# An attention kernel planned at build time: new times in its planner, a drain time between dependent passes, queued broadcasts, and a table of leads by query block

## The chip, the cores and the metric

The kernel runs on one core of a Trainium2 chip. The metric is the device time of one execution in microseconds (us). Before the change the median of three runs is 408.36 us (408.36 to 408.42).

## The reference

Multi-head attention over one sequence of 2048 tokens, 16 heads of 28 columns, bfloat16 inputs:

```python
B, S, D, H = 1, 2048, 448, 16
qkv = (lambda x, *d: x.transpose(*d))((x @ wqkv).reshape(B, S, 3, H, Dh), 2, 0, 3, 1, 4)
q, k, v = qkv[0], qkv[1], qkv[2]
scores = jnp.einsum("bhqd,bhkd->bhqk", q, k) * (Dh ** -0.5)
p = _softmax(scores, axis=-1)
o = jnp.einsum("bhqk,bhkd->bhqd", p, v)
return (lambda x, *d: x.transpose(*d))(o, 0, 2, 1, 3).reshape(B, S, D) @ wo
```

## The kernel before

**Tiling.** The heads form 4 groups of 4 (g), the queries 4 chunks of 512 (c), the keys 16 tiles of 128 (j). A *query block* w = 4g + c is one chunk of one group; there are 16. A *score tile* is 128 keys by 512 queries of one head; there are 16 x 16 x 4 = 1024. Four score tiles (the heads of a group) with the same j make a *row*. TensorE (PE) computes the scores transposed, keys on the partitions (`emit_S`, L868), so that the exponentials can be fed back as they are: for each row four matmuls with a 32-column weight, side by side in the array, add V times exp into the bank PO (`pv_op`, L1136). A column of ones in VA gives the softmax's sum. Instead of a row's maximum, a bound of it is folded into the scores with extra partitions of Q and K (KMAX, NK, KPART, QP).

**Three ways to an exponential.** PSUM has eight banks: two pairs PA (two tiles each), three single banks PD, and PO.
- ACT: two score tiles in a PA pair, one Exp over 1024 columns into PTA (L1291).
- DVE with GpSimd (POOL): one score tile in a PD bank; DVE makes DU (L1072) and DV (L1075), POOL the product DG (L1078), DVE adds it up to the bits of the exponential in PTD (L1091). The PD bank is free after the last of them. Here this is called a DVE tile.
- POOL alone: DVE copies the bank to SG (L1004), POOL does six operations on it (L1011 to L1034). There are 24 such tiles; `ahead` takes them from some rows ahead of the others.

**Other work between them.** PE also makes K (L525), Q (L656) and V (L727) of the next group or query block and the output projections (L810, L830, L902, L1430). DVE copies these from PSUM. DMAs on SP's queue copy Q and K to other partitions (QB<-QB, QB<-QP, KB<-KB) and broadcast the key bound (KB<-NK); after each query block the sums go out and come back as a broadcast (DCO, SCR, RRB), and POOL divides (OT, L971). At the start x is transposed on PE (L417) or by DMA, and copied to XT (L428, L430).

**What sets the order.** Nothing is ordered by hand. At build time the kernel plays its own execution through: every piece of work is an `Op` with an engine, a planned duration, a latency until others may use the result, dependencies, and a priority. A loop steps through planned time. For each engine it takes the next Op (`try_pe`, `try_act`, `try_static`) and appends it to a log, which then becomes the program: one fixed queue for each engine, whose instructions wait for semaphores at run time. So the planned durations decide the order, and also which score tile goes to ACT and which to DVE, since a tile goes to DVE whenever a PD bank is planned to be free. The real times are the chip's.

In `try_pe` the order of choice is: scores for ACT when a PA pair is free; a late projection; a score tile for DVE when a PD bank is free; a PV row; another projection; otherwise a matmul of zeros to keep PE busy. Each of the later choices must pass `fits`: it may not hold PE past the end of the running exp by more than `SLK`. A matmul of another family (scores, PV, projections) than the last is charged `MODE`.

```python
def fits(dur, fam):
    d = dur + (MODE if fam != last_fam[0] else 0.0) + (MODE if fam != "S" else 0.0)
    return not tight or not any(t < x and t + d > x + SLK for x in exp_ends)
```

Projections have a position of the score tiles from which they may run (`elig`), a priority (`due`), and one from which they may also take a PD bank (`urgent`). The constants `UK`, `UQ`, `LA`, `J0`, `O1`, `O2`, `OF`, `RV`, `GY`, `GS` and others give these leads, the same for all query blocks.

Of the kernel before, what the change touches and what calls it, by code (L numbers as in the profile page):

```python
# [10 lines left out]
ALU = mybir.AluOpType  # L11
# [10 lines left out]
G = 4  # L22
HG = 4
# [16 lines left out]

SEM = 0.13
MM = 0.22
MODE = 0.105
PLAT = 0.24
P1 = 0.598
TT5 = 0.33
TS5 = 0.2
PTT = 1.12
PTS = 0.59
PST = 1.125  # L50
CPY = 0.6
EVK = 0.66
RED = 0.59
DISS = 0.6
DLAT = 1.4
QLAT = 2.6
# [26 lines left out]
def kernel(  # L83
# [31 lines left out]
    UK = 30  # L115
# [3 lines left out]
    LA = 10  # L119
# [3 lines left out]
    GY = 0.5  # L123
    GS = 1.0
    GBEG = 40
    J0 = 10
    NTAIL = 8
    JL = 6
    JACC = 8
    DI = 1  # L130
    PVM = 0.0
    PLD = 0.2
    YIELD = 0
    SLAT = 0.5
    ASL = -0.05
    ELAT = 0.05
    PGAP = 0.03
    PFIN = 0.3
# [3 lines left out]
    RNGB = 6.2  # L142
    RNGN = 0.35
    J3 = 9
    UQ = 60
    OD = 2
    PADQ = 1
    O1 = 10
    O2 = 20
    OF = 0.4  # L150
    RV = 2
    QPR = 100
    LOOK = 0.2
    SLK = 0.13
    MG = 0.1
# [7 lines left out]
    UO = 40  # L163
    FB = TPC
    NF = 2
    J1 = 8
# [189 lines left out]

    def step():
        pos[0] += 1
        while pos[0] in taken:
            pos[0] += 1  # L360
# [26 lines left out]
    k0mm = []  # L387
    hot = []
# [13 lines left out]
    for b in range(NQC - XBAR):  # L402
        xs_in = add(Op("SP", 0.01, None, prio=-2000 + b, lat=XLAT[b]))
        for hf in range(2):
# [14 lines left out]
            tro = add(Op("PE", 0.55 if b else (0.75, 0.65)[hf], tr, deps=[xs_in], prio=(-1200 if b else -5000) + 10 * b + (hf ^ THF[b]), lat=PLAT, kind="T",  # L419
# [66 lines left out]
    k0mv = []  # L486
    m0 = Op("DVE", 0.0, None)
# [23 lines left out]
    def task_K(g, sc):  # L511
        due = g * 4 * WT - 200 + 36 * sc
# [5 lines left out]
        else:  # L518
            task = bank_task()
            acq = acq_d(task, urgent=(g - 1) * 4 * WT + (sc + 1) * KSP - UK)  # L520
            elig = at((g - 1) * 4 * WT + sc * KSP + 2)
            prio = due
        def ap():
# [3 lines left out]
                       (xt_done[sc] if g or sc else xt_done[0][:1]) + [w_ready[("k", g)]], prio, elig, acq, half=None if g or sc else xt_done[0][1:])  # L527
        if g == 0 and sc == 0:
            k0mm.extend(ops)
        cs = slice(sc * QW, (sc + 1) * QW)  # L530
        if g == 0:
# [18 lines left out]
            else:  # L550
# [6 lines left out]
                evs[0].acq = lambda t: red.start is None or red.done(t)  # L557
# [13 lines left out]
    def task_kmax(g):  # L571
# [7 lines left out]
        if g == 0:  # L579
            nk = add(Op("DVE", 0.2, lambda: nc.vector.tensor_scalar(  # L580
                out=NK[0][:], in0=maskm[:, 0:P], scalar1=KMAX[0][:, 0:1], scalar2=RK0[:, 0:1], op0=ALU.mult, op1=ALU.mult),
                deps=[m] + rk_op, prio=prio + 0.2))
            for n, (c0, c1) in enumerate(KCH):
                for i in range(HG):
# [3 lines left out]
                        deps=[k0ev[sc] for sc in range(c0, c1)], prio=-2000 + 20 * n + i, lat=DLAT + 0.3))  # L588
# [8 lines left out]
            for n, (c0, c1) in enumerate(RCH):  # L597
                for i in range(HG):
                    o = add(Op("SP", DISS + 0.07, (lambda i=i, c0=c0, c1=c1: rep0(i, c0, c1)), deps=[nk],
                               prio=(-1990 + 20 * n if c0 else -300) + 0.1 * i, lat=DLAT + 0.6, elig=None if c0 else lambda t: pos[0] >= NF * FB * HG + 4))  # L600
                    for c in range(c0, c1):
                        kmrep[(g, c, i)] = o
# [3 lines left out]
        for st in (1, 3):  # L606
            o = add(Op("SP", DISS, (lambda st=st: nc.sync.dma_start(
                out=KB[g % 2][1][HP * st:HP * (st + 1), c0 * QW:S], in_=KB[g % 2][0][HP * st:HP * (st + 1), c0 * QW:S])),
                deps=[kev[(g, sc, 0)] for sc in range(c0, NQC)], prio=due + 0.01 * st, lat=DLAT + 0.3))
# [11 lines left out]
        for i in (2, 3, 0, 1):  # L621
            o = add(Op("SP", DISS + 0.07, (lambda i=i: rep_out(i, c0)), deps=[nk] + ([deps[i]] if i < 2 else []),
                       prio=due + 0.3 + 0.001 * i, lat=DLAT + 0.6))
# [7 lines left out]
    def task_Q(g, c):  # L631
# [9 lines left out]
        else:  # L641
            task = bank_task()
            acq = acq_d(task, urgent=w * WT - UQ)
            elig = at((w - 1) * WT + 3 - (QEA if w > 3 else 0))
            prio = due - (QPR if w > 3 else 0)
# [71 lines left out]
    def task_V(g, jq):  # L717
        due = g * 4 * WT + jq * TPC * HG - 12 + (FB * HG * (NF - 1) if g == 0 and jq else 0)
        task = bank_task()
        early = False  # L720
        elig = at(VE + jq * 5 if g == 0 else (g - 1) * 4 * WT + jq * WT + 4)
# [8 lines left out]
        for jj in range(TPC):  # L730
            ops.append(add(Op("PE", 0.27, (lambda jj=jj: mm(jj)), deps=(xt_done[jq] + [wvin]) if jj == 0 else [ops[-1]],
                              prio=prio + 0.001 * jj, kind="W", elig=elig, acq=acq_d(task, early, urgent=due - UV if g == 0 else (g - 1) * 4 * WT + (jq + 1) * WT + 32) if jj == 0 else None,
                              lat=0.0 if jj < TPC - 1 else PLAT)))
# [9 lines left out]
        ev = add(Op(eng, 0.54, ev_fn, deps=[ops[-1]], prio=prio - (0 if early else 1000), elig=elig))  # L743
# [43 lines left out]
    def task_part(c, n):  # L787
        due = (12 + c) * WT - PARTD
# [678 lines left out]
```

## Time and profile before

| | |
|---|---|
| median of three runs | 408.36 us |
| the profiled execution, its own time | 408.52 us |
| its span, first to last instruction | 406.7 us |
| granted PE clock, mean | 0.999 |
| DVE passes L1072, L1075, L1091 | 158 each; mean 680, 681, 679 ns |
| POOL DG L1078 | 158, mean 1154 ns |
| copies to SG L1004 | 24, mean 682 ns |
| score matmuls L868 to PA, to PD | 842, 182 |
| PV matmuls L1136 | 1024 |
| busy: PE, DVE, ACT, POOL | 89%, 94%, 97%, 82% of the span |

How to read it: a group's line gives the source line, the engine, the operation and what is written from what is read, then the count, the busy time, the mean of one record and the idle time of the engine just before such instructions. Records of one engine overlap, because an engine begins an operation while the last one drains; the mean of one record is therefore longer than the step from one to the next. In a timeline the two numbers in front are the start and the length, both in us, and square brackets hold the engine's idle time before, with what ended it.

### The profile page before, as it was taken

The numbers are of one execution on the slowest core, as the hardware profiler recorded it, in microseconds if no ns is written. First come the engines' busy times: TensorE is split into PE (matmuls) and PEld (weight loads), VectorE is DVE, ScalarE is ACT, GpSimd is POOL, SyncE is SP. The second block draws the span as 40 slices with busy tenths as digits, with TensorE's granted clock in tenths as the row PEclk, the third lists the DMA queues.
The fourth block names the chain that finished last, engine by engine and source line by source line (L and its number), as shares of the span: only waits on it lengthen the run. The fifth ranks groups of instructions, "written<-read, shape, count | busy, mean of one in ns | idle before, by whom it ended". The sixth has DMA issues, their size and how long they took to land.

```text
span 406.7 us, 7593 instructions
## 1 busy us (share of the span) xinstructions
PE 362.2 (89%) x2606; PEld 121.4 (30%) x2606; DVE 381.5 (94%) x671; ACT 393.6 (97%) x432; POOL 331.5 (82%) x357
## 2 busy tenths in 40 slices
PE   8999888898998989899898989899898888989896
PEld 5243232323222222222323223232322222222232
DVE  6998999999999999989999998999989999999995
ACT  4989999999999999999999999999999999999994
POOL 4038799678699899998989898898898889999860
PEclk9999999999999999999999999999999999999999
DMA  9351130211400002100510000010130101000112
GB/s 219 44 86 39 48 76 3 50 27 28 96 5 27 19 24 35 16 25 6 110 30 27 23 4 26 2 47 21 48 59 15 35 1 46 22 20 10 47 73 90
DMA packets 36446, 16.58 MB, mean 41 GB/s; under 512 B 28784, under 2 KB 33136, under 8 KB 36408
## 3 DMA queue, kind: packets, MB, share of 16 engines
q1 hardware_dynamic: 35800, 15.89, 16.7%
q8 instruction: 20, 0.33, 0.3%
q10 hardware_dynamic: 608, 0.22, 0.2%
q14 instruction: 18, 0.15, 0.1%
HBM read 7.44 MB, written 1.97 MB: 23 GB/s over the span
## 4 chain that ended last, share of the span: by engine, by line
ACT 74%; PE 16%; issue 7%; DVE 1%; ACTq 0%
ACT PTA L1291 74%; PE PA L868 6%; PE PO L1136 4%; PE PD L868 1%; PE PD L810 1%; PE PA L396 1%; PE PO L810 1%; PE PD L417 1%; DVE DU L1072 0%; DVE DV L1075 0%; PE PO L525 0%; PE PD L525 0%; PE PA L417 0%; PE PD L902 0%; PE PD L656 0%
## 5 line engine op out<-in xcount | busy, mean ns | idle before, releaser
L1291 ACT ACTIVATE PTA<-PA 128x1024 bf16<-128x1024 f32 x421 | 386.6, 1222 | 1.3 <-PE PA L868 1.3
L1078 POOL TENSOR_TENSOR DG<-DV,DU 128x512 f16<-128x512 f16 x158 | 180.7, 1154 | 46.6 <-DVE DV L1075 36.5
L868 PE MATMUL PA<-QB,KB 64*128 64x512 bf16 x842 | 167.4, 380 | 38.2 <-ACT PTA L1291 35.6
L868 PEld LDWEIGHTS <-KB 64*128 64x128 bf16 x1024 | 67.6, 93 | 181.8 <-issue 174.1
L1072 DVE TENSOR_SCALAR DU<-PD 128x512 f16<-128x512 uint16 x158 | 104.9, 680 | 7.3 <-PE PD L868 6.8
L1091 DVE SCALAR_TENSOR_TENSOR PTD<-PD,DG 128x512 uint16<-128x512 f32 x158 | 106.5, 679 | 3.6 <-POOL DG L1078 2.7
L1075 DVE SCALAR_TENSOR_TENSOR DV<-PD,DU 128x512 f16<-128x512 uint16 x158 | 105.5, 681 | 1.0
L1136 PE MATMUL PO<-PTA,VA 128*32 128x512 bf16 x842 | 86.1, 386 | 0.0
L868 PE MATMUL PD<-QB,KB 64*128 64x512 bf16 x182 | 65.2, 377 | 0.6
L1136 PE MATMUL PO<-PTD,VA 128*32 128x512 bf16 x182 | 52.2, 387 | 0.0
L1136 PEld LDWEIGHTS <-VA 128*32 128x32 bf16 x1024 | 19.0, 94 | 47.6 <-issue 47.4
L1021 POOL TENSOR_TENSOR SG<-SG,GU 128x512 f32<-128x512 f32 x24 | 27.7, 1154 | 1.4 <-DVE QP L695 0.4
L1017 POOL TENSOR_TENSOR GV<-GE,GU 128x512 f16<-128x512 f32 x24 | 27.8, 1156 | 1.2
L1019 POOL TENSOR_TENSOR GU<-GV,GU 128x512 f16<-128x512 f16 x24 | 27.7, 1154 | 0.4
L971 POOL TENSOR_TENSOR OT<-OSB,RRB 128x512 bf16<-128x512 f32 x15 | 19.0, 1270 | 3.2 <-DVE DU L1072 2.4
L1011 POOL TENSOR_SCALAR GU<-SG 128x512 f16<-128x512 uint16 x24 | 14.8, 617 | 6.6 <-DVE SG L1004 3.0
L656 PE MATMUL PO<-XT,WQP 112*128 112x512 bf16 x56 | 18.7, 386 | 0.0
L1004 DVE COPY SG<-PD 128x512 f32<-128x512 f32 x24 | 16.4, 682 | 1.8 <-PE PD L868 1.8
L1014 POOL TENSOR_SCALAR GE<-SG 128x512 f32<-128x512 uint16 x24 | 14.8, 618 | 3.3 <-DVE QP L695 1.8
L525 PE MATMUL PO<-XT,WKP 112*128 112x512 bf16 x52 | 16.9, 385 | 0.0
L727 PEld LDWEIGHTS <-XT 112*128 112x128 bf16 x256 | 13.5, 98 | 10.5 <-issue 10.3
L1034 POOL TENSOR_SCALAR PTD<-SG 128x512 uint16<-128x512 f32 x24 | 14.8, 618 | 1.0
(108 smaller groups left out, 193.7 us busy)
## 6 DMA issues: line engine op xcount, KB each, us to landing
RRB<-SCR SPq DMA_DIRECT2D x15, 256.0 KB
QB<-QP SPq DMA_DIRECT2D x56, 32.0 KB
KB<-NK SPq DMA_DIRECT2D x12, 128.0 KB
XS<-in_x_dram SPq DMA_DIRECT2D x3, 448.0 KB
QB<-QB SPq DMA_DIRECT2D x28, 32.0 KB
out_dram<-XS SPq DMA_DIRECT2D x2, 448.0 KB
KB<-KB SPq DMA_DIRECT2D x6, 128.0 KB
RRB<-SCRF SPq DMA_DIRECT2D x2, 256.0 KB
```

Source lines behind the costliest of these rows:

```text
L656: ops = chain_mm(CC, lambda cc: nc.tensor.matmul(out=ap(), lhsT=WQP[g][:, cc, :], rhs=XT[c][cc // 2][0:CK, cc % 2, :], start=(cc == 0), st ...
L868: nc.tensor.matmul(out=ap, lhsT=KB[g % 2][i // 2][a:a + 64, j * P:(j + 1) * P], rhs=QB[w % NQB][i // 2][a:a + 64, :], start=True, stop=Tru ...
L971: o5 = add(Op("POOL", 1.22, lambda: nc.gpsimd.tensor_tensor(out=OT[g][c][:], in0=OSB[b][:], in1=RRB[b][:], op=ALU.mult), deps=o4, prio=-10 ...
L1017: g3 = add(Op("POOL", PTT, lambda: nc.gpsimd.tensor_tensor(out=GV[:], in0=GE[:], in1=GU[:], op=ALU.mult), deps=[g2], prio=prio + 2, kind=" ...
L1019: g4 = add(Op("POOL", PTT, lambda: nc.gpsimd.tensor_tensor(out=GU[:], in0=GV[:], in1=GU[:], op=ALU.mult), deps=[g3], prio=prio + 3, kind=" ...
L1021: g5 = add(Op("POOL", PST, lambda: nc.gpsimd.tensor_tensor(out=X[:], in0=X[:], in1=GU[:], op=ALU.add), deps=[g4], prio=prio + 4, kind="g", ...
L1072: p1 = add(Op("DVE", P1, lambda: nc.vector.tensor_scalar(out=DU[b][:], in0=lo, scalar1=SIG / 65536, scalar2=SIG * (SS - 0.5), op0=ALU.mult ...
L1075: p2 = add(Op("DVE", P1, lambda: nc.vector.scalar_tensor_tensor(out=DV[b][:], in0=lo, scalar=65536 * (SS - 0.5 + CE / C3), in1=DU[b][:], o ...
L1078: gq = add(Op("POOL", PTT, lambda: nc.gpsimd.tensor_tensor(out=DG[b][:], in0=DV[b][:], in1=DU[b][:], op=ALU.mult), deps=[p2], prio=n, kind ...
L1091: f = add(Op("DVE", P1, lambda: nc.vector.scalar_tensor_tensor(out=PTD[st["s"].idx][:].bitcast(U16), in0=PX[slot.idx][:], scalar=EBITS + C ...
L1136: nc.tensor.matmul(out=PO[HP * st:HP * (st + 1), :], lhsT=VA[g][:, j, st, :], rhs=r["p"][i][1](), start=first, stop=last, tile_position=(0 ...
L1291: nc.scalar.activation(out=PTA[pslot.idx][:, 0:len(ns) * QW], in_=PA[s.idx][:, 0:len(ns) * QW], func=ACT.Exp, bias=ACT_BIAS, scale=ACT_SCALE)
```

## The change

The planner's times are replaced (a pass of DVE or POOL, a copy, latencies after an operation). PE is no longer charged `MODE`; a table `PACE` holds the step from one family of matmul to another (S scores for ACT, s for DVE, V a PV row, F the others), and `pe_at` gives when the next could start. An Op of DVE may now follow an Op of DVE that it depends on after `WDR`, and POOL's pass behind the pass that it depends on is charged `TDEP`. A broadcast that is issued while another is under way is planned to land `RNG2` later. The leads are taken from `PLAN`, by query block (or by group and chunk); `now()` is the block in which planning stands. At the start, the copy of the last quarter of the first group's keys goes behind NK on DVE, the second half's KB<-KB copies go behind the first four broadcasts on SP, and zero matmuls into PD0 may stand ahead of the second quarter's K matmuls.

```diff
+PLAN = {
+    "PVROWS": [8, 10, 12, 13, 11, 3, 10, 12, 9, 10, 13, 4, 9, 10, 7, 6],
+    "AHEAD": [10, 10, 12, 10, 13, 5, 9, 5, 10, 15, 7, 13, 3, 9, 12, 10],
+    "LEAD1": [10, 9, 0, 20, 6, 15, 10, 12, 2, 13, 13, 41, 17, 9, 22, 45],
+    "LEAD2": [12, 28, 10, 27, 24, 61, 21, 21, 32, 25, 40, 27, 19, 12, -6, 43],
+    "LEAD3": [0.4, 10, 0.5, 0.6, -4, 0.3, 38, 19, -5, 44, 0.6, -4, 17, 2, 0, 24],
...
+    "TAIL": [8, 8, 40, 1],
...
+    "SLK": [0.2, 0.2, 0.26, 0.2, 0.2, 0.2, 0.12, 0.15, 0.18, 0.24, 0.2, 0.14, 0.15, 0.11, 0.2, 0.26],
+}
+
 SEM = 0.13
-MM = 0.22
-MODE = 0.105
-PLAT = 0.24
+MM = 0.2
+PACE = {"SS": 0.43, "Ss": 0.215, "SV": 0.32, "SF": 0.324, "sS": 0.262, "ss": 0.22, "sV": 0.303, "sF": 0.306,
+        "VS": 0.345, "Vs": 0.332, "VV": 0.226, "VF": 0.33, "FS": 0.37, "Fs": 0.31, "FV": 0.31, "FF": 0.216}
+TDEP = 0.12
+WDR = 0.117
+PLAT = 0.21
 P1 = 0.598
...
-PTT = 1.12
-PTS = 0.59
-PST = 1.125
-CPY = 0.6
-EVK = 0.66
-RED = 0.59
+PTT = 1.108
+PTS = 0.582
+PST = 1.108
+CPY = 0.598
+EVK = 0.657
+RED = 0.57
...
-QLAT = 2.6
+QLAT = 1.7
...
-    PLD = 0.2
+    PLD = 0.16
...
-    SLAT = 0.5
-    ASL = -0.05
-    ELAT = 0.05
-    PGAP = 0.03
-    PFIN = 0.3
+    SLAT = 0.39
+    ASL = 0.051
+    ELAT = 0.06
+    PGAP = 0.0
+    PFIN = 0.075
...
+    RNG2 = 2.9
...
-    MG = 0.1
+    SLK = 0.24
+    MG = 0.0
...
-                evs[0].acq = lambda t: red.start is None or red.done(t)
+                evs[0].acq = lambda t: (red.start is None or red.done(t)) and (sc < NQC - 1 or red.start is None or (nk0 and nk0[0].start is not None))
...
-                        deps=[k0ev[sc] for sc in range(c0, c1)], prio=-2000 + 20 * n + i, lat=DLAT + 0.3))
+                        deps=[k0ev[sc] for sc in range(c0, c1)], prio=-2000 + 20 * n + i, lat=DLAT + 0.3,
+                        elig=(lambda t: all(r.start is not None for r in rep0s[0:HG])) if n else None))
...
-            acq = acq_d(task, urgent=w * WT - UQ)
-            elig = at((w - 1) * WT + 3 - (QEA if w > 3 else 0))
-            prio = due - (QPR if w > 3 else 0)
+            acq = acq_d(task, urgent=w * WT - PLAN["QBY"][w])
+            elig = at((w - 1) * WT + 3 - (QEA if w > 3 else 0) - PLAN["QFROM"][w])
+            prio = due - (QPR if w > 3 else 0) - PLAN["QLEAD"][w]
...
-            deps=[sop] + prevl, prio=n - O1))
+            deps=[sop] + prevl, prio=n - PLAN["LEAD1"][now()], lat=WDR))
...
-            deps=[p1], prio=n - O2, lat=0.22))
+            deps=[p1], prio=n - PLAN["LEAD2"][now()], lat=0.157))
...
+    def pe_at(t, fam):
+        return max(t, pe_last[0] + PACE[last_fam[0] + fam])
...
-        late = MODE if last_fam[0] == "S" else 0.0
...
-            if s.free_at + late <= t + 1e-9 and pos[0] < NT and s_ready(pos[0], t) and s_ready(after(pos[0]), t):
+            if s.free_at <= pe_at(t, "S") + 1e-9 and pos[0] < NT and s_ready(pos[0], t) and s_ready(after(pos[0]), t):
...
-            d = dur + (MODE if fam != last_fam[0] else 0.0) + (MODE if fam != "S" else 0.0)
-            return not tight or not any(t < x and t + d > x + SLK for x in exp_ends)
+            u = pe_at(t, fam) + PACE[fam + "S"]
+            return not tight or not any(t < x and u > x + PLAN["SLK"][now()] for x in exp_ends)
...
-        if ready > RV or ready and pv_next[0] >= (NW - 1) * NKT:
+        if ready > PLAN["PVMORE"][now()] or ready and pv_next[0] >= (NW - 1) * NKT:
...
+        if t < 13.5 and fits(MM, "F") and kuse[0] and all(o.done(t) for o in kuse[0]) and k1op[0].start is None and activity(t) < BAR:
+            return Op("PE", MM, lambda: nc.tensor.matmul(out=PD[0][:], lhsT=zeros[:], rhs=zrow[:], start=True, stop=True), lat=PLAT, kind="K")
...
-            if all(d.done(t) for d in o.deps) and (o.acq is None or o.acq(t)):
+            if all(d.done(t) or d.eng == e and d.end is not None and d.end + WDR <= t + 1e-9 for d in o.deps) and (o.acq is None or o.acq(t)):
...
+                    if o.kind == "g" and (pool_last[0] in o.deps or o.dur == PTS and o.deps[0].eng == "DVE"):
+                        o.dur += TDEP
...
-                        ring[0] = t + RNGB
+                        if t < ring[0]:
+                            o.lat = max(o.lat, ring[0] + RNG2 - o.end)
+                            ring[0] += RNG2
+                        else:
+                            ring[0] = t + RNGB
```

The number of score tiles, what is computed in each, the buffers and the DMAs stay the same; their order, and which tile goes which way, are the new plan's.

## The prediction

> **What bounds the kernel now.** I read the page's first lines first, then the busy time in a long window of the middle, then ScalarE's (ACT's) timeline, the waits, and last the timelines of both ends.
>
> ```profile
> span 406.7 us, 7593 instructions
> PE 362.2 (89%) x2606; PEld 121.4 (30%) x2606; DVE 381.5 (94%) x671; ACT 393.6 (97%) x432; POOL 331.5 (82%) x357
> ...
> L1291 ACT ACTIVATE PTA<-PA 128x1024 bf16<-128x1024 f32 x421 | 386.6, 1222 | 1.3 <-PE PA L868 1.3
> ```
>
> The 421 exps of ACT (two score tiles each, 842 of the 1024) hold 386.6 us, with 1.3 us of idle time before them in all. The middle shows how full it is:
>
> ```profile
> 28.00:398.00 370.00, 331.33 (x2397) 108.02 (x2396) 354.35 (x607) 370.00 (x405) 323.66 (x320) 1.00 0.14 33
> ```
> ```profile
> 179.41 21.45 ACT L1291 ACTIVATE PTA<-PA 128x1024 bf16<-128x1024 f32 x23
> ...
> 199.58 21.46 ACT L1291 ACTIVATE PTA<-PA 128x1024 bf16<-128x1024 f32 x23
> ```
>
> In the first row (PE, PEld, DVE, ACT, POOL) ACT is busy 370.00 of 370 us. The two stretches of 23 share one exp, so 22 exps take 199.58 - 179.41 = 20.17 us: one per 0.917 us, although a single record lasts 1.222 (they overlap). Time is therefore: when the first exp starts, plus 0.917 per exp, plus holes in ACT, plus what follows the last exp. DVE (354.35 of 370) is nearly as full; POOL has 46 us free.
>
> ```profile
> PE PA L868 <- ACT PTA L1291: 35.6, 107, 0.5
> ...
> DVE DU L1072 <- PE PD L868: 6.8, 14, 1.1
> ```
>
> PE waits for ACT to free a PA bank, not the other way round. DVE's idle time is mostly waiting for a score tile.
>
> **A, fewer exps: -2.75.** The built order of instructions is the plan's result and is fixed. It has 418 exps instead of 421, 164 DU, DV, DG and PTD passes instead of 158, and the same 24 tiles through SG. So 3 x 0.917 = 2.75 us leave ACT. [...]
>
> **B, the first exp: +0.98 (0.55 to 1.0).**
>
> ```profile
> 9.14 0.61 PE L417 MATMUL PO<-ident,XS 128*112 128x128 bf16 x8
> ...
> 9.52 0.28 DVE L678 COPY QB<-QB 128x512 bf16<-128x512 bf16 x1
> ...
> 9.84 1.48 DVE L682 TENSOR_SCALAR QB<-QP,KPART 32x512 bf16<-32x512 bf16 x4
> 9.93 0.79 ACT L541 ACTIVATE KB<-PD,bndcol,selcol 128x512 bf16<-128x512 f32 x1
> ...
> 10.24 1.50 PE L868 MATMUL PA<-QB,KB 64*128 64x512 bf16 x4
> ...
> 11.02 13.86 ACT L1291 ACTIVATE PTA<-PA 128x1024 bf16<-128x1024 f32 x15 [0.30 <-PE PA L868]
> ...
> 12.15 0.67 DVE L428 COPY XT<-PO 112x1024 bf16<-112x1024 bf16 x1
> ```
>
> The first scores need the four small L682 passes, and the first exp starts 11.02 - 9.84 = 1.18 after these begin. In the new order DVE copies XT<-PO (now at 12.15) before them. It can't start before its transposes end (9.14 + 0.61 = 9.75) and holds DVE 0.6: at least 10.4 - 9.84 = +0.55. Two K matmuls also go behind one Q matmul more, 0.22 later for the KPART reduce. A second chain is longer: three new zero matmuls on PD0 stand ahead of the first scores in PE's queue, and PD0 is read by ACT's KB pass until 9.93 + 0.79 = 10.72. Zeros at 10.74, two further steps of 0.23, 0.37 from them to the scores: 11.57, and 0.43 to the exp (24.99 to 25.44 below is 0.45): 12.00. I take 12.00 - 11.02 = +0.98.
>
> **C, the early holes: -0.84 (-1.25 to 0).**
>
> ```profile
> 24.99 0.41 PE L868 MATMUL PA<-QB,KB 64*128 64x512 bf16 x2
> ...
> 25.44 1.02 ACT L1291 ACTIVATE PTA<-PA 128x1024 bf16<-128x1024 f32 x1 [0.56 <-PE PA L868]
> ...
> 26.93 9.27 ACT L1291 ACTIVATE PTA<-PA 128x1024 bf16<-128x1024 f32 x10 [0.47 <-PE PA L868]
> ```
>
> These two exps end 1.586 and 1.494 after the one before; over 0.917 that is 1.25 lost. PE was late: between 23.09 and 24.99 its queue has V, three v groups and two V. An exp that ACT stood waiting for ends 25.44 + 1.02 - 24.99 = 1.47 after its scores start, an ordinary one 1.78, so scores may be 0.31 to 0.33 late for nothing. I added up the steps of each cycle from one score pair to the next in the new order (S to V 0.32, row to row of V 0.23, V to S 0.35, S to a projection 0.32, one projection matmul to the next 0.23, from it to S 0.37, S to s 0.22, s to S 0.26, all medians of this trace), and carried what is over 0.917 forward. The old order gives holes at these same two exps; the new one leaves 0.10, 0.24 and 0.08 within the first 27 exps: 0.41 instead of 1.25. From the 28th exp to the last no carried lateness reaches 0.33, though 29 cycles now pass 1.0 us (10 before). On SP the first four broadcasts (KB<-NK) now go ahead of all four copies KB<-KB of the second half, one of which stood before them; NK goes ahead of the last key copy on DVE. The moved copy is issued four issues of 0.67 = 2.7 later and lands near 26 instead of 22.98; its keys are first read by the 25th exp, past 33, and the exps before it hide that. If a broadcast were late instead, C would be 0.
>
> **D, after the last exp: +0.43 (0 to 0.6).**
>
> ```profile
> 397.16 0.39 PE L868 MATMUL PA<-QB,KB 64*128 64x512 bf16 x2
> ...
> 399.14 0.40 PE L1136 MATMUL PO<-PTA,VA 128*32 128x512 bf16 x4
> ...
> 399.60 0.72 DVE L880 STREAM_TRANSPOSE SG<-PO 128x512 f32<-128x512 f32 x1
> ```
>
> Everything to the end hangs on the last PV row (L1136), 1.98 after the last scores. The new order has five rows and three WO matmuls behind them: 0.32 + 3 x (0.33 + 0.29) + 0.23 = 2.41, so +0.43. If the last PTD pass, now behind two XS adds, ends last, it is 2.56: +0.6. If the last exp decides, 0.
>
> **E, the middle: +0.5 (0 to 4.3, the first rival; not below 0, since ACT has no hole there to give back).** Six more tiles are 18 DVE passes, each 0.60:
>
> ```profile
> 390.93 1.28 DVE L1072 TENSOR_SCALAR DU<-PD 128x512 f16<-128x512 uint16 x2
> ...
> 393.32 0.68 DVE L1072 TENSOR_SCALAR DU<-PD 128x512 f16<-128x512 uint16 x1
> ...
> 394.04 0.69 DVE L1075 SCALAR_TENSOR_TENSOR DV<-PD,DU 128x512 f16<-128x512 uint16 x1
> ```
>
> 1.28 for two records of 0.68 is a step of 0.60; a DV straight behind its own DU starts 0.72 after it. So 18 x 0.60 = 10.8 more, in a middle 2.75 shorter: 13.5 us of DVE's 370 - 354.35 = 15.65 idle must go. Twelve fewer DV stand straight behind their DU (17, was 29): 12 x 0.12 = 1.4 back, so 12.1 of 15.65. The cover that hides the 10.8 is that idle time alone. What does not fit delays the PTD that frees a PD bank, then the score matmul on it, then the score pair queued behind that on PE, then ACT. The planner's new constants agree with rows here to about 0.01 (0.598 per pass, 0.755 from DV to DG where I find 0.756, 1.183 from DG to PTD where I find 1.181), which is why I take the low end and not none: 0.5. QB copies are planned to land 1.7 after issue; without a broadcast ahead they take 1.3, so no wait of their own is added. POOL's six DG (6 x 1.15 = 6.9) lie in its 46 free us.
>
> The Trainium skill has a rule against the drain part: chained DVE ops pay the pipe's drain regardless, with or without semaphores (VectorE: DVE Perf Modes, The DRAIN you can't avoid). The rows disagree, 0.72 against 0.60. By the rule 0 instead of 1.4 would come back, 13.5 of 15.65 would be needed, and E would be nearer 1.
>
> **Sum:** -2.75 + 0.98 - 0.84 + 0.43 + 0.5 = -1.68. The profiled execution took 408.52 (span 406.7 and 1.8 around it): 406.84. The runs' median is 408.36, 0.16 below: 406.7. With every term at its low end, E at 0, -3.45 gives 404.9.
>
> **Rivals.** *DVE runs out of room (slower).* Its idle time is many short waits; if only half of it can be filled, 12.1 - 7.8 = 4.3 us are missing and become holes in ACT in place of E: 406.2 + 4.3 = 410.5. It decides from the point where less than 10 of the 15.65 can be used (then 2.1 are missing, 408.3). For it: 12.1 of 15.65 is a lot. Against: POOL DG waits 36.5 us for DV, so the chain DU, DV, DG, PTD has slack on POOL's side.
> *The gain is eaten by lateness on PE.* The 29 cycles over 1.0 us leave a margin of 0.33; if a DVE or POOL wait inside one cycle in four makes 0.2 of hole each, 1.4 is lost beside E: 408.1, no change. Against: ACT never waited in the middle.
> *The start is not delayed.* If the zeros find PD0 free and the copy slips into a gap, B is 0: 405.7.
>
> **Chances.** Forecast 0.54 (404.9 to 407.5), start not delayed 0.13, eaten 0.13, DVE out of room 0.20. The bound of what can be told from no change is 0.2%, 0.82 us: faster means below 407.54. Faster 0.54 + 0.13 = 0.67, same 0.13, slower 0.20. The range 404.9 to 409.9 takes in half of the DVE rival.
>
> **What would show it.** A: 418 exps, 0.917 apart. B: first exp near 12.0, with XT<-PO ahead of L682's passes. C: no idle time over 0.3 before an exp between 20 and 30 us. D: the last PV row 2.4 after the last scores. E: ACT at 369 or more of 370 in the middle, DVE near 99%. Wrong if ACT shows idle time behind PD banks that DVE holds, many times over the middle, or if DVE idles as much as before while ACT waits.

## The result and the profile after

The changed kernel takes 412.24 us in the median of five runs (410.61 to 413.08). The kernel before took 408.36 beside it. The ratio is 1.0094, with a 95% interval of 1.0068 to 1.0119: slower by about 3.9 us, where 406.7 was forecast. The profiled execution is the quickest of the five, 410.61 us. In all five the mean granted PE clock was 0.991 to 0.994.

These are lines from the page of the changed kernel:

```profile
span 408.8 us, 7595 instructions
...
PE 363.2 (89%) x2619; PEld 117.3 (29%) x2619; DVE 389.8 (95%) x689; ACT 391.7 (96%) x429; POOL 338.4 (83%) x363
...
L1326 ACT ACTIVATE PTA<-PA 128x1024 bf16<-128x1024 f32 x418 | 384.7, 1145 | 5.3 <-PE PA L897 4.3
```

There are three exps fewer, as planned, but ACT's idle time before them grew from 1.3 to 5.3 us. The table of windows of the same kernel shows where, in the columns PE, PEld, DVE, ACT, POOL, then the granted PE clock:

```profile
28.00:398.00 370.00, 330.68 (x2400) 103.73 (x2398) 360.48 (x621) 366.07 (x400) 328.35 (x324) 1.00 0.14 33
46.56:48.85 2.29, 0.39 (x3) 0.10 (x2) 0.74 (x2) 1.78 (x2) 2.29 (x3) 1.00 0.09 35
49.12:52.53 3.41, 3.41 (x25) 0.60 (x24) 3.36 (x6) 1.63 (x2) 3.41 (x5) 0.50 0.02 5
```

In the long middle ACT lacks 3.93 us of 370, where it lacked nothing before. At 46.56 there are 2.29 us in which PE works for 0.39 and DVE for 0.74 while POOL is busy all the time. Right behind it the PE clock is granted at half for 3.41 us, and ACT works for 1.63 of these. The timeline of that place, read from top to bottom:

```profile
45.69 1.27 POOL L973 TENSOR_TENSOR OSB<-OSB,RRB 128x512 f32<-128x512 f32 x1 [2.19 <-DVE SG L1033]
...
46.56 0.39 PE L897 MATMUL PA<-QB,KB 64*128 64x512 bf16 x2
46.92 1.15 POOL L1107 TENSOR_TENSOR DG<-DV,DU 128x512 f16<-128x512 f16 x1
...
48.10 0.69 DVE L1120 SCALAR_TENSOR_TENSOR PTD<-PD,DG 128x512 uint16<-128x512 f32 x1 [2.07 <-POOL DG L1107]
...
48.85 0.37 PE L897 MATMUL PD<-QB,KB 64*128 64x512 bf16 x1 [1.90 <-DVE PTD L1120]
...
49.70 0.61 PE L897 MATMUL PA<-QB,KB 64*128 64x512 bf16 x2
...
50.41 1.03 ACT L1326 ACTIVATE PTA<-PA 128x1024 bf16<-128x1024 f32 x1 [2.08 <-PE PA L897]
```

POOL's multiply of the first query chunk's partial sums (`finish_block`) waits 2.19 us. The view puts the wait down to DVE's SG copy, which had ended at 45.44. By the trace's transfer records the broadcast RRB landed at 45.21, and POOL's sequencer ended its wait for that transfer at 45.25, 0.44 before the multiply began. In zeros_in_pause and before_pool_earlier below, where this multiply stood waiting for over 2 us too, it began 0.48 and 0.47 after RRB's landing, as it did here (0.48). So it waited for RRB. Behind the multiply in POOL's queue stands a DG whose input DV had been ready since 44.24. It runs at 46.92; its PTD, the score tile that needs the PTD's bank, the score pair behind that tile in PE's queue, and the exp follow one after the other. In the kernel before, the two multiplies stand further back in POOL's queue, behind a DG and two operations on an SG tile, and start without a wait:

```profile
43.95 1.15 POOL L1078 TENSOR_TENSOR DG<-DV,DU 128x512 f16<-128x512 f16 x1 [0.70 <-DVE DV L1075]
...
47.01 2.49 POOL L944 TENSOR_TENSOR OSB<-OSB,RRB 128x512 f32<-128x512 f32 x2
```

The exps 39 to 42 (counted from 0) end 3.25 us later in all than at a step of 0.917 (2.19, 0.60, 0.31 and 0.16). Why the broadcast is late shows in SP's queue:

```profile
33.75 3.76 SPq L739 DMA_DIRECT2D QB<-QP  x4
37.60 0.67 SPq L962 DMA_DIRECT2D SCRF<-RR  x1
39.41 1.21 SPq L963 DMA_DIRECT2D RRB<-SCRF  x2
```

The broadcasts read SCRF, so they can't be issued before its transfer has landed: 39.41, 1.81 after the issue of SCRF. The plan made at build time has SCRF at 35.42 and the broadcast at 36.04, only 0.62 later. SCRF's own 2.18 of lateness has the same form. Two of the four QB<-QP ahead of it, the first two, may not overwrite what the two QB<-QB read; the plan has them from 33.02 on in one row with these, and in the run the first went at 33.75 and the second at 35.73, when the QB<-QB had landed (33.69 and 35.71; the second took 2.69 from the end of its issue, the first 1.30). Together the broadcast is issued 39.41 - 36.04 = 3.37 late. It comes in the main from one line of the change:

```diff
-            if all(d.done(t) for d in o.deps) and (o.acq is None or o.acq(t)):
+            if all(d.done(t) or d.eng == e and d.end is not None and d.end + WDR <= t + 1e-9 for d in o.deps) and (o.acq is None or o.acq(t)):
```

`try_static` plans DVE, POOL and SP. For a DVE pass behind a DVE pass, "0.117 us after its end" is a drain time. For SP "its end" is the end of the issue, not the landing, so the same words let a transfer read what another transfer has not written yet. The program is still right, since it waits for semaphores; only the plan believes in an earlier time. The plan of the changed kernel has its last exp at 396.05 and the run at 400.62, 4.6 late. Before, the plan had 400.54 and the run 398.91, 1.6 early.

### The profile page after: what moved, and what is told of

The parts are those of the page before. It is cut to its first block, busy times and chain, and to the rows that moved or that the text cites. A ratio compares the mean times of both kernels' runs of the same rounds, so it can differ in the third digit from the quotient of the medians.

```text
span 408.8 us, 7595 instructions
## 1 busy us (share of the span) xinstructions
PE 363.2 (89%) x2619; PEld 117.3 (29%) x2619; DVE 389.8 (95%) x689; ACT 391.7 (96%) x429; POOL 338.4 (83%) x363
## 4 chain that ended last, share of the span: by engine, by line
ACT 50%; DVE 18%; PE 18%; issue 8%; POOL 3%; DMA 2%; SPq 0%; DVEq 0%; ACTq 0%
ACT PTA L1326 49%; PE PA L897 6%; DVE DU L1101 5%; DVE DV L1104 4%; PE PO L1165 4%; DVE PTD L1120 4%; PE PD L897 2%; POOL DG L1107 2%; DMA KB<-KB 1%; PE PO L549 1%; PE PA L418 1%; DVE KB L587 1%; PE PD L549 1%; DVE SG L1033 1%; DVE QB L695 1%
## 5 line engine op out<-in xcount | busy, mean ns | idle before, releaser
L1107 POOL TENSOR_TENSOR DG<-DV,DU 128x512 f16<-128x512 f16 x164 | 187.4, 1156 | 43.9 <-DVE DV L1104 37.4
L1120 DVE SCALAR_TENSOR_TENSOR PTD<-PD,DG 128x512 uint16<-128x512 f32 x164 | 110.8, 682 | 5.7 <-POOL DG L1107 4.6
L897 PEld LDWEIGHTS <-KB 64*128 64x128 bf16 x1024 | 62.7, 93 | 181.6 <-issue 171.8
L1101 DVE TENSOR_SCALAR DU<-PD 128x512 f16<-128x512 uint16 x164 | 108.8, 681 | 1.8 <-PE PD L897 1.3
L1104 DVE SCALAR_TENSOR_TENSOR DV<-PD,DU 128x512 f16<-128x512 uint16 x164 | 109.0, 681 | 0.6
L897 PE MATMUL PD<-QB,KB 64*128 64x512 bf16 x188 | 69.1, 377 | 5.8 <-DVE PTD L1120 3.0
L1165 PE MATMUL PO<-PTD,VA 128*32 128x512 bf16 x188 | 57.1, 390 | 0.2 <-DVE KB L587 0.2
L756 PE MATMUL PO<-WV,XT 112*128 112x112 bf16 x224 | 17.1, 214 | 0.2
```

The source lines that it names most:

```text
L897: nc.tensor.matmul(out=ap, lhsT=KB[g % 2][i // 2][a:a + 64, j * P:(j + 1) * P], rhs=QB[w % NQB][i // 2][a:a + 64, :], start=True, stop=Tru ...
L1101: p1 = add(Op("DVE", P1, lambda: nc.vector.tensor_scalar(out=DU[b][:], in0=lo, scalar1=SIG / 65536, scalar2=SIG * (SS - 0.5), op0=ALU.mult ...
L1104: p2 = add(Op("DVE", P1, lambda: nc.vector.scalar_tensor_tensor(out=DV[b][:], in0=lo, scalar=65536 * (SS - 0.5 + CE / C3), in1=DU[b][:], o ...
L1107: gq = add(Op("POOL", PTT, lambda: nc.gpsimd.tensor_tensor(out=DG[b][:], in0=DV[b][:], in1=DU[b][:], op=ALU.mult), deps=[p2], prio=n, kind ...
L1120: f = add(Op("DVE", P1, lambda: nc.vector.scalar_tensor_tensor(out=PTD[st["s"].idx][:].bitcast(U16), in0=PX[slot.idx][:], scalar=EBITS + C ...
L1165: nc.tensor.matmul(out=PO[HP * st:HP * (st + 1), :], lhsT=VA[g][:, j, st, :], rhs=r["p"][i][1](), start=first, stop=last, tile_position=(0 ...
```

## Experiments

Theories: the *queue theory* (this rule on SP makes broadcasts late against the plan, a waiting instruction holds a queue, and the PE clock falls behind the pause), the *DVE theory* (VectorE has no room for the six tiles more, the rival of the prediction) and the *clock theory* (the clock falls by itself). Ratios are to the kernel before on the same chip, in brackets the 95% interval.

| run | median us | ratio | last exp, profiled | holes in ACT after 40 us |
|---|---|---|---|---|
| changed kernel | 412.24 | 1.0094 [1.0068, 1.0119] | 400.62 | 5.11 |
| pool_later | 409.12 | 1.0023 [1.0014, 1.0031] | 399.00 | 3.14 |
| pool_later_2 | 408.11 | 0.9992 [0.9984, 1.0001] | 397.81 | 2.28 |
| zeros_in_pause | 410.45 | 1.0069 [1.0042, 1.0097] | 400.74 | 5.05 |
| before_pool_earlier | 409.23 | 1.0018 [1.0009, 1.0026] | 399.27 | 1.01 |
| before_sp_early | 413.81 | 1.0132 [1.0097, 1.0168] | 404.04 | 5.54 |
| plan_late_broadcast | 424.26 | 1.0375 [1.0350, 1.0401] | 414.52 | 17.62 |
| plan_sp_waits | 425.91 | 1.0422 [1.0406, 1.0437] | 416.54 | 23.75 |
| pool_2_and_head | 407.27 | 0.9970 [0.9959, 0.9981] | 397.29 | 2.23 |
| spare_pta | 406.85 | 0.9970 [0.9959, 0.9982] | 397.00 | 1.89 |
| spare_pta_and_sp_order | 406.27 | 0.9954 [0.9942, 0.9967] | 395.87 | 1.40 |
| more_dve_work | 416.81 | 1.0223 [1.0191, 1.0254] | 406.05 | 11.31 |
| du_twice | 412.46 | 1.0097 [1.0081, 1.0114] | 402.37 | 7.27 |

The last column is my sum, over the intervals between the ends of exps that are over 0.93 us, of what is over 0.917. The kernel before has 0.14.

### pool_later and pool_later_2: the multiply further back in POOL's queue

```diff
     log.sort(key=lambda e: (e[0], e[1]))
+    behind(pool[k0], rest[1])
+    behind(pool[k1], rest[3])
```

`pool` is POOL's planned order, k0 and k1 the places of the two multiplies, `rest` the order from the first multiply on without the two; `behind` moves an Op in the log. This is pool_later; pool_later_2 has rest[0] and rest[2].

> The changed kernel; only POOL's order differs: the two multiplies OSB<-OSB,RRB stand behind two and behind four of the passes that they stood ahead of. Every other queue is as in the changed kernel, 418 exps too. Queue theory (the multiply waits 2.19 us in POOL's queue for the RRB broadcast, holds a DG, that holds a PTD, that a score tile, and the TensorE clock falls to half for 3.41 us behind the pause): the holes before exps 39 to 42 (3.25 us at 49 to 55 us) vanish, no half clock before the tail, 410.6 - 3.25 = 407.4 us. DVE theory (VectorE has no room): DVE has the same 331 us of work between 60 and 398 us, so the time stays near 410.6 and the holes only move. Clock theory (the gate falls by itself since less TensorE work is planned): the drop near 49 us stays, and with it about 1 us; 408.4.

> The changed kernel; in POOL's queue the two multiplies OSB<-OSB,RRB stand behind one and behind three of the DG passes that they stood ahead of, which is where their broadcasts land (45.2 and 47.9 us). In the first such run, with them one and two places later still, the holes at 49 us went but others of 1.26 us came at exps 44, 47, 50, 55 and 64, where DVE waited 0.4 to 0.5 for DG passes that ran 1.1 us later. Queue theory: those go too, 409.1 - 1.26 = 407.9 us, and no half clock. DVE theory: they are DVE's lack of room and stay: 409.1.

The first gave 409.12 instead of 407.4: the pause went, and so did the half clock (1.00 in the windows), but the DG passes that the multiplies now held back caused holes of their own. The second put each multiply where its broadcast lands, and gave 408.11 against the 407.9 expected. POOL and ACT in its timeline:

```profile
44.35 1.15 POOL L1107 TENSOR_TENSOR DG<-DV,DU 128x512 f16<-128x512 f16 x1 [0.82 <-DVE DV L1104]
45.70 1.27 POOL L973 TENSOR_TENSOR OSB<-OSB,RRB 128x512 f32<-128x512 f32 x1 [0.19 <-DMA RRB<-SCRF]
46.93 2.30 POOL L1107 TENSOR_TENSOR DG<-DV,DU 128x512 f16<-128x512 f16 x2
49.19 1.27 POOL L973 TENSOR_TENSOR OSB<-OSB,RRB 128x512 f32<-128x512 f32 x1
```
```profile
42.42 7.78 ACT L1326 ACTIVATE PTA<-PA 128x1024 bf16<-128x1024 f32 x8
```

The multiply starts at 45.70, where it started before; but the DG now runs ahead of it at 44.35, and ACT goes through without a hole. Nothing but the place of two instructions in one queue differs from the changed kernel, and it is worth 4 us (1.0094 to 0.9992). The holes of the two profiled runs differ by 2.83; the rest is not in the changed kernel's profile, which was of its quickest run.

### zeros_in_pause: what the clock costs by itself

```diff
+    def zeros_more():
+        for _ in range(8):
+            nc.tensor.matmul(out=PO[:], lhsT=zeros[:], rhs=zrow[:], start=False, stop=False, skip_group_check=True)
+    k = [k for k, e in enumerate(log) if e[2].kind == "s"][13]
+    log.insert(k, (log[k][0], log[k][1], Op("PE", 8 * MM, zeros_more, kind="K")))
```

> The changed kernel with eight matmuls of zeros added to PO's open sum in TensorE's queue, ahead of the score tile at 48.85 us that waits 1.90 us: TensorE is kept busy for 8 x 0.215 = 1.7 us of its pause, and nothing else changes. Queue theory: the wait itself (hole of 2.19 before exp 39) stays, the clock does not fall at 49.1, so the later part of the hole (0.595 + 0.31 + 0.163 = 1.07) goes: 409.5. If the clock does not follow the pause: no change, 410.6. If the whole loss came from the clock: 407.4.

The timeline and one window of this kernel:

```profile
46.71 1.27 POOL L973 TENSOR_TENSOR OSB<-OSB,RRB 128x512 f32<-128x512 f32 x1 [3.07 <-DMA RRB<-SCRF]
...
47.29 1.67 PE L1448 MATMUL PO<-zrow,zeros 128*128 128x512 bf16 x7 [0.16 <-issue]
...
49.12 0.69 DVE L1120 SCALAR_TENSOR_TENSOR PTD<-PD,DG 128x512 uint16<-128x512 f32 x1 [2.95 <-POOL DG L1107]
```
```profile
49.00:53.00 4.00, 3.13 (x34) 0.77 (x35) 3.84 (x7) 2.01 (x3) 4.00 (x5) 1.00 0.01 4
```

In this run the broadcast landed later still and the pause was longer (3.07 instead of 2.19; here the view does name RRB). Even so the clock stayed at 1.00 behind it, and the holes of exps 40 and 41 went. Five of its seven runs had a mean clock of 0.999 or 1.000, where none of the changed kernel's five was over 0.994; the other two (0.992 and 0.988) are its slowest, 412.87 and 414.25. So the clock falls because PE has too little to do in the pause, and the clock theory is ruled out. The Trainium skill (TensorE: Matmul & The Clock Gate, What's actually happening) has PE's gate halve the clock by the activity of a free-running window of 3413 ns. The traces agree: in the changed kernel the half clock lasted 3.413 us, and in plan_late_broadcast below such stretches begin at 211.49, 259.28 and 313.89 us, 14 and 16 times 3.413 us after one another. They do not agree with the idle window that the same section asks for: in the 3.41 us before the clock fell in the changed kernel PE was busy for 1.44. What the half clock costs in time is less sure: the ratios 1.0094 and 1.0069 differ by 1.0 us, and their intervals overlap. In the profile it is at most the 1.07 behind the first hole.

### before_pool_earlier: the same fault put into the kernel before

```diff
     log.sort(key=lambda e: (e[0], e[1]))
+    ahead_of(pool[k0], pool[k0 - 3])
+    ahead_of(pool[k1], pool[k0 - 2])
```

> The kernel before, with the changed kernel's fault alone: in POOL's queue the two multiplies OSB<-OSB,RRB (at 47.01 and 48.23) are put ahead of the DG that ran at 43.95 and behind that one. 421 exps, all else as before. The first broadcast lands at 44.24 and the multiply starts near 44.7, so that DG starts near 46.0, 2.0 late. Queue theory: a hole of 1 to 2.5 us in ScalarE near 47 to 50 us, perhaps with half clock behind it: 408.4 + 1 to 3.3 = 409.4 to 411.7. DVE theory: the kernel before has 4 to 5 us more of idle DVE and takes the delay up: 408.4.

The multiply waited 2.01 us and the DG started at 45.96, as expected, but the hole was only 0.73 us, there was no half clock at that place, and the time rose by 0.8 (ratio 1.0018): less than the queue theory's 1 to 3.3, more than the DVE theory's nothing. The old order takes up most of a DG's delay of 2.0 us; a delay of 2.6 (46.92 here, 44.35 in pool_later_2) costs the new one 3.25, the part behind the half clock included. How much a late transfer costs seems to depend on what slack stands behind it. Since the two delays also differ in size, that the new order has less slack is not shown by this pair.

### before_sp_early and plan_sp_waits: the rule alone, and the change without it

```diff
-            if all(d.done(t) for d in o.deps) and (o.acq is None or o.acq(t)):
+            if all(d.done(t) or e == "SP" and d.eng == e and d.end is not None and d.end + 0.117 <= t + 1e-9 for d in o.deps) and (o.acq is None or o.acq(t)):
```

for the kernel before, and for the changed one `d.eng == e != "SP"` in place of `d.eng == e`. Both are planned anew.

> The kernel before with one thing of the change alone: its planner lets an SP transfer that depends on an earlier SP transfer be issued 0.117 us after the end of that one's issue, and no longer only when that one has landed. All other rules and durations are the old ones; the new plan has 421 exps as before and its last exp at 400.80 (before: planned 400.54, run 398.91, 1.63 earlier than planned). Theory that this rule is the fault: waits come that the plan does not have, as for RRB, and the run falls behind the plan: last exp past 401, 410.5 us or more. Theory that the rule is harmless alone, and the change's tight DVE and POOL order turns it into a loss: 408.4 to 409.

> The changed kernel planned anew with the early start withdrawn for SP alone (DVE and POOL keep it), the table of leads unchanged. The plan has 415 exps and its last exp at 415.1, with 23 us of planned holes (9.9 of them at 194, 4.1 at 290 us): the table was made for the planner with the fault. Theory that the fault on SP is what makes the run later than the plan (4.6 us in the changed kernel, 13 in the one with later broadcasts): here run and plan agree, last exp 413.5 to 416, 423 to 426 us. If other mis-sized steps make it late: 428 us or more.

The rule alone makes the old kernel 5.4 us slower (ratio 1.0132), with 421 exps and every duration as it was. Its run is 3.2 behind its plan (404.04 to 400.80), where the old one was 1.6 ahead. The worst place, in its timeline:

```profile
289.51 0.54 SPq L968 DMA_DIRECT2D RRB<-SCR  x1
...
290.15 1.24 SPq L704 DMA_DIRECT2D QB<-QB  x2
...
294.56 2.41 SPq L710 DMA_DIRECT2D QB<-QP  x4
...
297.01 1.22 SPq L607 DMA_DIRECT2D KB<-KB  x2
...
299.43 2.71 SPq L617 DMA_DIRECT2D KB<-NK  x4
...
304.21 0.39 PE L868 MATMUL PD<-QB,KB 64*128 64x512 bf16 x2 [2.59 <-DMA KB<-NK]
...
304.92 1.02 ACT L1291 ACTIVATE PTA<-PA 128x1024 bf16<-128x1024 f32 x1 [1.91 <-PE PA L868]
```

The plan has the first QB<-QP at 290.43, right behind the two QB<-QB. These land at 294.51, behind the broadcast, and so it goes at 294.56, 4.1 late, and the keys' transfers were placed behind it. It holds KB<-KB, that holds KB<-NK, and PE waits 2.59 us for its keys; behind that pause the clock is at half for 3.413 us too, from 305.24. It is the same fault as at 45 us in the changed kernel, in another queue.

plan_sp_waits ran 1.4 behind its plan (416.54 to 415.11) and took 425.91, inside the expected 423 to 426 us, though the last exp was past the expected 413.5 to 416. Without the rule on SP the lateness against the plan falls from 4.6 to 1.4. Part of that could be the plan's own holes, which take up lateness, but at the place of the fault it has none, and in the run no exp from 37 to 77 ends over 0.93 us after the one before. SP's queue there, to be held against the changed kernel's above:

```profile
33.16 3.30 SPq L739 DMA_DIRECT2D QB<-QP  x4
36.55 0.68 SPq L962 DMA_DIRECT2D SCRF<-RR  x1
38.36 1.20 SPq L963 DMA_DIRECT2D RRB<-SCRF  x2
```

The plan has these two broadcasts at 37.92, so the first is 0.44 late instead of 3.37. It is also issued 1.05 earlier than in the changed kernel, because the two QB<-QP that wait for no QB<-QB now go first. The time itself says that the table `PLAN` holds only for the planner that it was made with: one corrected line moves 23 us of holes into the plan.

### plan_late_broadcast: one lead corrected

```diff
-            deps=[d], prio=-10, lat=GLAT)) for w in range(NF)]
+            deps=[d], prio=-10, lat=GLAT + 2.0)) for w in range(NF)]
```

> The changed kernel, planned anew with one lead corrected: the two broadcasts RRB<-SCRF are planned to land 2.0 us later (8.5 instead of 6.5 us after the issue), which is what the run showed them late by. The plan then has 419 exps, one more, and a last exp at 401.3 instead of 396.05, with 5.5 us of planned holes where the table of leads was made for the other plan. Queue theory: no pause at 49 us and no half clock there; one exp more is +0.92; whether the planned holes come about is open: 408.3 if none does, up to 413 if all do. DVE theory: about as the changed kernel, 410 to 412.

It took 424.26, above every figure expected, and ran 13.2 behind its own plan, with SP's rule still in force. Its largest unplanned holes stood behind waits of PE for SP's transfers: KB<-NK at 210 and 312 us (1.7 and 2.1 on a score matmul), QB<-QP at 258 (1.6). The expected end of the pause near 49 us did not come either: the second multiply waits 2.05 us for its broadcast there, and a hole of 1.66 follows.

```profile
49.27 1.27 POOL L973 TENSOR_TENSOR OSB<-OSB,RRB 128x512 f32<-128x512 f32 x1 [2.05 <-DMA RRB<-SCRF]
```

A single lead was not mended by planning anew with this table; moving two instructions in the finished order did it.

### pool_2_and_head: the start

```diff
+    copy = next(o for _, _, o in log if o.eng == "DVE" and o.prio == -680)
+    behind(copy, rk_op[0])
+    log[:] = [e for e in log if not (e[2].kind == "K" and 10.6 < e[0] < 11.2)]
```

> The run above with the head put back: on DVE the copy XT<-PO goes behind the four L711 passes that write the first scores' QB, and the three matmuls of zeros on PD0 ahead of the first scores are left out. If the first exp is late for those two (the reading of the prediction), it starts 0.7 to 0.85 us earlier against the start of the L711 chain. Theory that a late start is a plain loss: 407.9 - 0.8 = 407.1. Theory that start and early holes are one account (what the exps gain at the start, they lose again before exp 16, where TensorE is late with the V projections whatever the start): the holes before exps 15 and 16 grow from 0.2 to about 1.0, and the time stays at 407.9.

407.27 against 407.1 and 407.9: the start is a plain loss (0.84 by the medians), and the hole before exp 16 did not grow (0.13). The changed kernel's start and this one's, each from its timeline:

```profile
8.00 0.69 ACT L699 ACTIVATE QB<-PD,offscol 128x512 bf16<-128x512 f32 x1 [1.75 <-PE PD L685]
...
9.67 0.69 DVE L450 COPY XT<-PO 112x1024 bf16<-112x1024 bf16 x1
...
10.32 0.81 PE L1275 MATMUL PD<-zrow,zeros 128*128 128x512 bf16 x3 [0.25 <-ACT KB L567]
...
11.57 1.94 ACT L1326 ACTIVATE PTA<-PA 128x1024 bf16<-128x1024 f32 x2 [1.30 <-PE PA L897]
```
```profile
8.39 0.69 ACT L699 ACTIVATE QB<-PD,offscol 128x512 bf16<-128x512 f32 x1 [1.84 <-PE PD L685]
...
11.18 1.02 ACT L1326 ACTIVATE PTA<-PA 128x1024 bf16<-128x1024 f32 x1 [0.52 <-PE PA L897]
```

The inputs land at other times in other runs, so the start is counted from the first QB pass: 3.57 in the changed kernel, 2.79 here; before it was 11.02 - 8.45 = 2.57.

### spare_pta and spare_pta_and_sp_order: two smaller waits

```diff
+            pt = NPA if act_i[0] - 1 in (78, 105, 182, 208, 286) else pslot.idx
...
+    late_bc = next(o for o in sp if o.prio == -10 and 289.3 < o.start < 289.4)
+    behind(late_bc, [o for o in sp if 728 < o.prio < 728.1][-1])
```

> The kernel pool_2_and_head with a 25th PTA buffer, into which exps 78, 105, 182, 208 and 286 write (a buffer each time long free); nothing else is moved. In that run these five lost 0.05, 0.59, 0.26, 0.25 and 0.07, 1.21 us together, and the view names PE's PO, L1165 (PV rows) as what ended ACT's wait at exp 105. Theory that they wait for a PTA buffer which the PV rows still read (24 buffers are too few for the new order): all five holes go, 407.3 - 1.2 = 406.1. Rival, DVE: the holes come from late score tiles: no change, 407.3.

> The kernel spare_pta, and on SP the broadcast RRB<-SCR that was issued at 291.0 goes behind the two copies KB<-KB that stood behind it. There PE's score tile waited 0.65 us at 300 us for KB<-NK, the fourth of a row of transfers that all ran behind this broadcast's 5.3 us landing (it was planned at 289.34, before the transfer of SCR that it depends on had landed at 290.94). SP-rule theory: KB<-KB lands 4 us sooner, KB<-NK can be issued when NK is ready (295.1 instead of 296.7), the hole before exp 313 (0.40) goes or shrinks: 405.7. Rival: KB<-NK lands behind the broadcast in any order, and the hole stays: 406.1.

The wait for a PTA buffer, in pool_2_and_head, reads like this:

```profile
109.22 3.77 ACT L1326 ACTIVATE PTA<-PA 128x1024 bf16<-128x1024 f32 x4 [0.48 <-PE PO L1165]
```

ACT waits not for scores (PA) but for PV rows (PO) that still read the buffer it is to write. With a 25th buffer the holes at exps 182, 208 and 286 are gone, the one at 78 too, and the one at 105 is 0.06; 0.83 of new ones came at exps 107, 116, 211, 233, 241, 264 and 265. The ratio stayed at 0.9970, and the median of 406.85 does not reach the expected 406.1: the cause was named rightly, the gain was not.

The order on SP, in spare_pta and then in spare_pta_and_sp_order:

```profile
290.75 0.58 SPq L997 DMA_DIRECT2D RRB<-SCR  x1
291.37 1.20 SPq L636 DMA_DIRECT2D KB<-KB  x2
296.44 2.73 SPq L646 DMA_DIRECT2D KB<-NK  x4
```
```profile
289.19 1.15 SPq L636 DMA_DIRECT2D KB<-KB  x2
290.45 0.58 SPq L997 DMA_DIRECT2D RRB<-SCR  x1
294.20 2.70 SPq L646 DMA_DIRECT2D KB<-NK  x4
```

KB<-NK is issued 2.24 sooner and the hole before exp 313 (0.38) is gone. This last kernel takes 406.27, above both figures expected (405.7 and 406.1), at a ratio of 0.9954 to the kernel before. Its interval overlaps that of spare_pta, so the gain of 0.6 between the two is not told apart from noise.

### more_dve_work and du_twice: how much room DVE has

```diff
+    first = [e for e in log if e[2].eng == "DVE" and e[2].lat == WDR and 60 < e[0] < 380]
+    for e in first[8::16]:
+        log.insert(log.index(e), (e[0], e[1], Op("DVE", P1, lambda f=e[2].fn: f() and None)))
```

(du_twice; more_dve_work has passes on constants instead, at nine other places.)

> The kernel pool_2_and_head with nine passes more on DVE (512 elements a lane, on constants, result unused), one every 64 DVE instructions between 70 and 380 us; DVE was busy 314.2 of the 320 us from 60 to 380 us there. If DVE still has room (each pass goes into the idle time near it): 407.3 to 407.8. If DVE is the bound (the rival 'DVE runs out of room'): nine passes of 0.3 to 0.6 us come out as holes, 410 to 412.7.

> The kernel pool_2_and_head with nine DU passes issued twice on DVE (same input, same output, read from PSUM, so that POOL's passes aren't slowed by them as the bf16 passes of the run before were: five of those nine took 1.1 to 1.6 us), every 16th between 60 and 380 us: 9 x 0.60 = 5.4 us more. In the run before, the four passes that took 0.62 to 0.68 cost 1.27 us of holes together, about half of their length. If DVE has room: 407.3 to 407.8. If half of each finds room: 407.3 + 2.7 = 410.0. If DVE is the bound: 412.7.

more_dve_work doesn't answer cleanly. Five of its nine passes took 1.11 to 1.60 us and the other four 0.62 to 0.68, so the work added was 9.3 us and not 5.4, for 9.5 us of time. Its profiled run also has two stretches of 3.413 us at half clock (from 151.70 and 230.21 us). The Trainium skill (GPSIMD Engine Reference, 1. Specifications) says that VectorE and GpSimd share their SBUF interfaces and contend when a DVE instruction has two SBUF inputs, as these had; the long ones agree with that, and so does what stands beside three of the other four: there the POOL operation that began second was longer instead (1.48, 1.73 and 1.64 us, where such operations take 1.15 to 1.27). No run here tests it by itself. du_twice is cleaner: 5.4 us more work, 412.46, 5.2 more time. Its profiled run has one stretch at half clock (from 340.96), but the run of 412.45 had a mean clock of 1.000. The windows from 60 to 380 us of the kernel before, of pool_2_and_head and of du_twice, in this order:

```profile
60.00:380.00 320.00, 285.12 (x2051) 91.43 (x2049) 308.79 (x529) 320.00 (x350) 285.53 (x285) 1.00 0.13 29
```
```profile
60.00:380.00 320.00, 283.16 (x2056) 89.25 (x2065) 314.17 (x541) 318.85 (x348) 286.52 (x284) 1.00 0.13 31
```
```profile
60.00:380.00 320.00, 282.78 (x2032) 87.21 (x2031) 314.76 (x542) 315.73 (x342) 281.70 (x280) 0.99 0.13 31
```

The third column of busy times is DVE's. The change took it from 308.8 to 314.2 of 320; with nine passes more it is 314.8, and ACT has lost its time instead (its fourth column, 318.85 to 315.73). None of the 5 to 6 us that are left idle took in the passes at these nine places. In this order DVE has no room left there: what is added comes out as time. Each added pass also holds up its own tile, and no run tells the two apart.

## Why the prediction was wrong

**The terms,** in the profiled execution (span 406.7 to 408.8, +2.1, forecast -1.68):

| term | forecast | measured |
|---|---|---|
| A, three exps fewer | -2.75 | -2.75 (418, step 0.917) |
| B, first exp | +0.98 | +0.55; +1.00 from the first QB pass |
| C, early holes | -0.84 | -1.06 |
| D, after the last exp | +0.43 | +0.40 (7.80 to 8.20) |
| E, middle | +0.5 | +4.97 |

**A** and **D** came as worked out, **C** 0.22 better and within its range. **B** was right in size, 1.00 us counted from the QB pass, and in the main in mechanism: with the copy XT<-PO and the zeros on PD0 put back (pool_2_and_head) 0.22 of it is left, so these two cost 0.78. The span shows 0.55 only because in that run this pass began 0.45 earlier (8.00, before 8.45). The rival "start not delayed" falls with it.

**E is the step that failed,** and in it one sentence: that QB copies "are planned to land 1.7 after issue", take 1.3, and "no wait of their own is added". The 1.3 held for the first of the two QB<-QB ahead of the broadcast and not for the second (2.69). Its landing came 35.71 - (33.02 + 1.7) = 0.99 later than the planned latency gives, a part of the 3.37 by which the broadcast is late. The larger part is that the new rule lets SP's dependent transfers go without any latency. The sentence looked at planned latencies, and the change's description ahead of the prediction reads that rule as one for DVE alone. Neither the text nor a rival says what happens on SP, though the rule's code compares engines and names none. What the runs showed in its place is a late broadcast, a multiply too early in POOL's queue, a pause on PE and half a clock: 3.25 of the 4.97. Putting two multiplies back gives 4 us of the median; the rule alone costs the old kernel 5.4. Of the other 1.7, 1.16 stand at the five exps that wait for a PTA buffer and 0.37 at the one behind KB<-NK.

**The rival "DVE runs out of room"** gave 410.5, near the 410.61 of the profiled run, but that is luck, since its mechanism was not the cause: in the pause DVE idles 1.55 of 2.29 us, and pool_later_2 does the same DVE work without the loss. Its premise was nearer than the forecast thought, though. It was to decide where less than 10 of the 15.65 us of DVE's idle time could be used. In pool_2_and_head DVE is busy 363.40 of the 370 us from 28 to 398, so 9.05 were used, and in du_twice no more of it took in added work. That most of what spare_pta took away came back as other holes fits it. Part of the 2.3 us of holes left in pool_later_2 after 40 us may be this rival; which part is not shown. E without the fault would have been nearer 2 (2.28 less the 0.14 of the kernel before) than 0.5.

**"Eaten by lateness on PE"** didn't come: of the 5.11 us of holes after 40 us in the changed kernel, 4.78 stand at the places just named, and 0.24 more at exp 36, whose two scores use the same half of PE's rows and start 0.22 apart (that this is its cause was not tried).

**Open:** how much of the median belongs to the clock (1.0 us by the ratios, not told apart from nothing); and why the other four runs of the changed kernel are 1.5 to 2.5 slower than the profiled one. Their clocks (0.991 to 0.994) and the spread of RRB's landing (the multiply started at 45.69 in the changed kernel's profile and at 46.71 in that of zeros_in_pause, whose order is the same up to there) point to longer pauses, but no profile of such a run was taken.

## What to carry to other kernels

When a planner's rule is loosened, go through every engine that the rule reaches, and ask for each what "end" means there: for an engine that computes, the result follows within a drain time (a pass of DVE starts 0.72 after the one that it reads, an independent one 0.60); for a queue that issues transfers, it follows at the landing, 1.1 us (SCRF) to 5.2 us (RRB) after the issue has ended here. An instruction put too early into a queue stops all that stands behind it: the two multiplies cost 4 us here. Put a little too late, in pool_later, the same two cost 1 us. And compare planned with measured ends: a run 4.6 us behind its plan shows the fault before any wait is read.

## What was not expected of the hardware

A pause of 2.3 us in which PE worked for 0.39 was enough for 3.413 us at half the granted clock; eight matmuls of zeros in the pause (1.7 us of work) prevented it in the profiled run. It seems to depend on where the pause falls: in plan_late_broadcast PE paused for 2.26 us from 50.17 and the clock stayed at 1.00. Counted back from its later falls in steps of 3.413, that pause is cut by a window's edge at 51.07, and PE was busy for 2.52 and 1.96 us of the windows on its two sides; the window before the fall in the changed kernel had 1.44. A 128x512 DVE pass with two bf16 inputs from SBUF took 0.62 to 1.60 us beside POOL's work, while the passes that read PSUM stayed at 0.68.
